# Weight conversion order, zero fillers, 384-token tiles and a new instruction order in a fused attention and two-MoE kernel

## The chip, the cores and the metric

The kernel runs on one core of a Trainium2 chip. The metric is the device time of one execution in microseconds, as the median of several runs. Smaller is better.

## What is computed

Four batches of eight heads of block-causal attention (sequence 576, head size 64, blocks of 64) feed a product chain without a nonlinearity, and that feeds an ELU layer:

```python
scores = where(block_i >= block_j, q @ k.T / 8, -1e9)     # 4 x 8 heads, 576 x 576
x  = softmax(scores) @ v                                  # laid out as 2304 tokens x 512
y  = ((x @ w1) * (x @ w2)) @ w3 @ w_out                   # w1, w2: 512x1024, w3: 1024x1024, w_out: 1024x512
h  = y @ w_in                                             # 512 x 2048
out = where(h > 0, h, exp(min(h, 0)) - 1) @ moe2_w_out    # 2048 x 512
```

Weights arrive as float64 words and are turned into float32 on the core.

## The kernel before, in words

**Numbers.** Most products run in a reduced float32 form on TensorE. Each operand is split into a high part and a rest, and three matmuls (`PASSES`) stand for one product. Two products use whole float32: the transposes of the probabilities, and `w3 @ w_out`.

**Conversion.** `convert` (line 309) turns one unit of 128 x 512 float64 words into float32: a DMA into a raw slot (`cr`, four slots in the first stage), two ScalarE instructions (c0 and c1, lines 354 and 347), three on VectorE (c2, c3, c4, lines 360, 363 and 368), and one on GpSimd (c5, line 377) that writes the finished unit `full`. Units of w1 and w2 get two more instructions that make the two parts. In the first stage there are 8 units of w_out (`wo`), 16 of w3 (`w3T`, two halves for each of 8 row blocks) and 16 of w1 and w2 (`w12`).

**Attention** (line 451). One pair of heads at a time, 16 pairs. A pair loads q, k and v, splits q and k, and has five row groups: scores `s` on TensorE (line 549, the last 64 rows at 611), a maximum on VectorE (570), an exponential on ScalarE (575), transposes `t` on TensorE (585, 645, 654), copies `pt` out of PSUM (439 or 440), and the products with v, `o`, on TensorE (675). The row sums go through a small DRAM buffer `scr` and come back spread over the partitions as `rr` (line 717), by which GpSimd scales the result in `xy` (729, the tile's "n" key).

**The product w3 @ w_out** (`w_product`, line 737). Eight row blocks i of eight terms j each, in PSUM bank 6 or 7. A term is one call of matmul, two matmul records in the trace. Term j of row i waits for both halves of w3's unit i and for both halves of w_out's unit j // 2.

**Block 2** (`block2`, line 776) is the first MoE layer, in 8 tiles of 288 tokens, half a batch each. A tile splits its x into `xs`; for each of 8 m it makes `a` and `b` (line 846, 12 matmuls each, in chunks of 6), multiplies them into `af` (863), and splits that into `g` (769 and 772). After m = 2, 5 and 7 (`PARTS`) the products with the finished w3 @ w_out are added into `xy` (810, copied out at 824 and 830). The first three tiles use one PSUM bank each for a, b and y (5, 6, 7); later tiles use two each, which they share with attention's banks (0, 1 and 3), and so wait until attention is through with these.

**Block 3** (`block3`, line 903) is the ELU layer, in 6 tiles of 384 tokens; `h` at line 918, `o` at 953. Its weights are converted while block 2 runs, once attention's buffers are free (`gate1`, `gate2`).

**The order** is not written by hand. Each instruction group is given to `Plan.add` with an engine, an assumed length and a priority. `Plan.run` walks through time with these lengths: at each step, of the engines' ready groups, it issues the one that can start earliest, with the lowest priority number among equals. The issue order of each engine's queue comes from that, and the chip then runs each queue in order. `TURNS` holds priorities of single groups that replace the usual ones. Usual priorities: the first four pairs -2500, w_out -3000, w3 -1000 + i, w3 @ w_out -2400 + i, w1 and w2 -992, later pairs 10 times their number, block 2 from 10000 on, block 3 from 100000 on; copies out of PSUM near -10000.

**Fillers** (line 1051). Until the first term of w3 @ w_out, `Plan.run` puts matmuls of the mask `mk`, into an unused tile `spare` of bank 6, wherever it sees TensorE idle for longer than 0.3 us: one for each 0.22 us. `mk` is zero but for parts of two rows.

Of the kernel before, what the change touches and what calls it, by code (L numbers as in the profile page):

```python
# [8 lines left out]
F32 = mybir.dt.float32  # L9
# [11 lines left out]
P = 128  # L21
WHOLE = 0
ADDED = 4
HS = 512
T2 = 288
T3 = 384
BIG = 2.0**100
PARTS = ((0, 1, 2), (3, 4, 5), (6, 7))
# [13 lines left out]
COL = 13 / 12 / 2400  # L42
# [166 lines left out]
def attention_moe_moe2(  # L209
# [21 lines left out]
    N2, N3 = B * S // T2, B * S // T3  # L231
# [93 lines left out]
    def convert(src, dst, keys, prio, first):  # L325
# [56 lines left out]
        def c7(eng):  # L382
# [5 lines left out]
            "ACT", 0.68, lambda: c0(nc.scalar), r=[rk], w=[t], prio=prio,  # L388
            ways=[("DVE", 0.42, lambda: c0(nc.vector), True)],
        )  # L390
        add("ACT", 0.68, c1, r=[rk], w=[rk2], prio=prio)
        add(
            "DVE", 0.42, lambda: c2(nc.vector), w=[t], prio=prio, port=True,
        )
        if ps:
            add("DVE", 0.67, c3, r=[t], w=[ps], prio=prio)
            add("DVE", 0.7, c4, r=[rk, ps], w=[t], prio=prio)
        else:
            add("DVE", 0.42, c3, w=[t], prio=prio, port=True)
            add("DVE", 0.7, c4, r=[rk], w=[t], prio=prio, port=True)  # L400
        if len(keys) == 1:
            add("POOL", 1.28, c5, r=[rk2, t], w=keys[0], prio=prio, port=True)
            return
        add("POOL", 1.28, c5, r=[rk2], w=[t], prio=prio, port=True)
        add("ACT", 0.61, lambda: nc.scalar.copy(dst(0), f()), r=[t], w=keys[0], prio=prio)
        add(
            "POOL", 1.28, lambda: c7(nc.gpsimd), r=[t, *keys[0]], w=keys[1], prio=prio, port=True,
# [14 lines left out]
    rr_r = Ring(pool1, "rr", 2, [P, S], F32)  # L422
# [21 lines left out]
    def attention(n, first_op):  # L444
# [42 lines left out]
        else:  # L487
            add("ACT", 0.67, lambda: nc.scalar.copy(qs()[:, 0, :], raw()[:, 0, :]), r=[(raw, 0)], w=[(qs, 0)], prio=pr)
            add(
                "ACT", 0.67,  # L490
# [9 lines left out]
                "DVE", 0.75,  # L500
# [30 lines left out]
        def group(g, seq):  # L531
# [7 lines left out]
            def scores():  # L539
# [20 lines left out]
                "PE", (4 * w / 2390 if whole else 3 * w * COL) + (0.25 if added else 0.12), scores,  # L560
                r=[*q_keys, *k_keys, "mask"], w=[*sb], prio=pg,
            )
            for h in range(2):
# [3 lines left out]
                def top(s=s, c=c):  # L567
# [4 lines left out]
                add("DVE", dve_us(nk) + (0.0 if added else 0.2), top, r=[s], w=[s, (st, "nm", c)], prio=pg)  # L572
                add(
                    "ACT", 0.47 + nk * 0.00083,
# [21 lines left out]
        def last_block(seq):  # L596
# [4 lines left out]
            for g in range(2):  # L601
# [26 lines left out]
                "DVE", 0.16, lambda: nc.vector.tensor_tensor(out=nm(10), in0=nm(8), in1=nm(9), op=ALU.min),  # L628
                r=[(st, "nm", 8), (st, "nm", 9)], w=[(st, "nm", 10)], prio=pg,
            )  # L630
            for g in range(2):
                add(
                    "ACT", 0.47 + kw * 0.00083,
                    lambda g=g: nc.scalar.activation(
                        out=p()[:, g * kw:(g + 1) * kw], in_=sb[g]()[:, 0:kw], func=AF.Exp, bias=nm(10), scale=1.0,
                        accum_out=sm(8 + g),
                    ),
                    r=[sb[g], (st, "nm", 10)], w=[(p, g), (st, "sm", 8 + g)], prio=pg,
                )
# [22 lines left out]
        def pv(c, seq):  # L662
# [20 lines left out]
            add("PE", (0.8, 2.15)[c], product, r=r, w=[o], prio=pg)  # L683
# [21 lines left out]
        add("DVE", 0.75, recip, r=[(st, "rest"), *((st, "sm", c) for c in range(10))], w=[(st, "rs"), rs], prio=pr + 6)  # L705
# [30 lines left out]

    def w_product(i, prio):
        ps = turn("w", (6, 7), "wps")
        for j in range(KF):

            def mm(j=j):
                plan.filler = None
# [13 lines left out]
        add("ACT", 0.58, lambda: nc.scalar.copy(d()[:, 0, :], ps()), r=[ps], w=[k[0]], prio=-9e3)  # L756
        add(
            "DVE", 0.68,
# [16 lines left out]

    def block2(t):
        b, h2 = divmod(t, 2)
        c0 = T2 * h2
# [3 lines left out]
        x = xy[b]  # L782
        for k in range(KD):
            src = lambda k=k: x()[:, k, c0:c0 + T2]
            add(
                "DVE", 0.32, lambda k=k, src=src: nc.vector.tensor_copy(xs()[:, k, 0, :], src()),
                r=[(x, k, "n")], w=[(xs, k, 0)], prio=fast, port=True,
            )
            add(
                "POOL", 0.79,  # L790
                lambda k=k, src=src: nc.gpsimd.tensor_tensor(
                    out=xs()[:, k, 1, :], in0=src(), in1=xs()[:, k, 0, :].bitcast(F32), op=ALU.subtract
                ),
                r=[(x, k, "n"), (xs, k, 0)], w=[(xs, k, 1), (x, k, "s", h2)], prio=fast, port=True,
            )
        gs = []
        few = t < 3
# [3 lines left out]
        def y_part(part):  # L801
            ms = PARTS[part]
            for n in range(KD):
                ps = turn("y" + nm_, ybanks, "y")
                for m in ms:

                    def mm(m=m, n=n, ps=ps):
                        w = wsl(W_S + m // 2).rearrange("p s (j c) -> p s j c", c=DM)[:, :, m % 2, :]
                        for q, (a, c) in enumerate(PASSES):
                            nc.tensor.matmul(  # L810
                                ps()[:, 0:T2], lhsT=w[:, a, n * P:(n + 1) * P], rhs=gs[m]()[:, c, :],
                                start=(m == ms[0] and q == 0), stop=(m == ms[-1] and q == 2),
                            )

                    add(
                        "PE", 3 * T2 * COL + 0.01, mm,
                        r=[(gs[m], 0), (gs[m], 1), *((slab_buf[W_S + m // 2], y, m % 2) for y in range(2))],
                        w=[ps], prio=base + (46, 90, 95)[part] + n, lag=0.5, big=True,
                    )
                d = lambda n=n: x()[:, n, c0:c0 + T2]  # L820
                dk = (x, n, "y", h2)
                if part == 0:
                    add(
                        "ACT", act_us(T2), lambda d=d, ps=ps: nc.scalar.copy(d(), ps()[:, 0:T2]),
                        r=[ps], w=[dk, (x, n, "s", h2)], prio=fast,
                    )
                else:
                    add(
                        "DVE", dve_us(T2),
                        lambda d=d, ps=ps: nc.vector.tensor_tensor(out=d(), in0=ps()[:, 0:T2], in1=d(), op=ALU.add),  # L830
                        r=[ps], w=[dk], prio=fast,
                    )
# [279 lines left out]
```

## Time and profile before

| what | value |
|---|---|
| median of 3 runs | 970.86 us (969.94 to 971.44) |
| profiled execution, own time | 971.84 us |
| its span, first to last instruction | 970.1 us |
| TensorE busy, matmul | 960.6 us (99%) |
| VectorE, ScalarE, GpSimd busy | 511.3, 427.6, 399.2 us |
| mean granted TensorE clock | 0.998 of 2.4 GHz |

Matmuls overlap in their pipeline, so a busy TensorE is not necessarily one that does useful or full-speed work: the mean length of a matmul record holds its latency. How often matmuls start one after the other is read from the start times, or from the length of a long piece of one kind in the chain of waits divided by its count.

### The profile page before, as it was taken

To read this page: it belongs to the slowest core of one execution; us is meant where nothing else is said; L and a number is where in the kernel's file an instruction comes from. 1 tells how busy PE (TensorE), PEld (TensorE's weight loads), DVE (VectorE), ACT (ScalarE), POOL (GpSimd) and SP (SyncE) were. 2 spreads that over 40 slices of the span, in tenths; PEclk is the share of its full clock that TensorE was granted. 3 is DMA by queue.
4 is the path that set the end of the run, shared out by engine and by line. 5 is a ranking of instruction groups with operands and counts; after the bars stand their busy time and mean duration, and the time that the engine had idled before them with its cause. 6 is when DMAs were issued, how large, how long until landed. Compare 5 with 4: busy or idle time off the path is not lost.

```text
span 970.1 us, 15899 instructions
## 1 busy us (share of the span) xinstructions
PE 960.6 (99%) x5910; PEld 821.4 (85%) x5910; DVE 511.3 (53%) x1087; ACT 427.6 (44%) x1008; POOL 399.2 (41%) x419
## 2 busy tenths in 40 slices
PE   9999999999999999999999999999999999999998
PEld 4555478788888889999999999998999889888997
DVE  7888988766565556676766342322322322322322
ACT  5867577556656654464454422222222222222222
POOL 6354758323232226666656542332322422422222
PEclk9999999999999999999999999999999999999999
DMA  8554433131122003245465950000000000000000
GB/s 290 195 184 161 160 128 96 54 96 50 50 78 71 27 16 112 95 154 183 171 210 202 391 233 1 1 32 1 23 12 1 25 10 1 33 1 1 33 1 33
DMA packets 41789, 87.61 MB, mean 90 GB/s; under 512 B 6000, under 2 KB 15472, under 8 KB 40176
## 3 DMA queue, kind: packets, MB, share of 16 engines
q1 hardware_dynamic: 41712, 86.60, 25.8%
q8 instruction: 46, 0.75, 0.3%
q14 instruction: 31, 0.25, 0.1%
HBM read 69.21 MB, written 17.38 MB: 89 GB/s over the span
## 4 chain that ended last, share of the span: by engine, by line
PE 93%; DVE 4%; DMA 1%; issue 1%; SPq 1%; POOL 0%; ACT 0%; POOLq 0%; DVEq 0%; ACTq 0%
PE h L918 21%; PE o L953 21%; PE b L846 10%; PE a L846 10%; PE y L810 10%; PE o L675 5%; PE s L549 4%; PE t L585 4%; PE wps L745 4%; PE spare L1054 3%; PE s L611 1%; DVE ct L368 1%; DVE ct L360 1%; PE t L645 1%; DMA scr<-rs 0%
## 5 line engine op out<-in xcount | busy, mean ns | idle before, releaser
L772 POOL TENSOR_TENSOR g<-e,g 128x384 fp32r<-128x384 f32 x96 | 97.4, 1016 | 276.6 <-ACT g L769 262.8
L930 DVE TENSOR_SCALAR e<-h 128x384 f32<-128x384 f32 x96 | 53.4, 557 | 221.6 <-PE h L918 210.1
L953 PE MATMUL o<-slab_lo,g 128*128 128x512 f32 x648 | 162.9, 396 | 0.0
L934 ACT ACTIVATE e<-e 128x384 f32<-128x384 f32 x96 | 50.4, 525 | 232.2 <-DVE e L930 232.2
L953 PEld LDWEIGHTS o<-slab_lo,g 128*128 128x128 f32 x648 | 121.1, 188 | 23.5
L810 PE MATMUL y<-g,slab_lo 128*128 128x288 f32 x768 | 118.9, 300 | 0.5 <-DVE xy L830 0.3
L846 PE MATMUL a<-xs,slab_lo 128*128 128x288 f32 x768 | 117.9, 298 | 0.0
L846 PE MATMUL b<-xs,slab_lo 128*128 128x288 f32 x768 | 117.1, 297 | 0.4 <-DVE af L863 0.4
L810 PEld LDWEIGHTS y<-g,slab_lo 128*128 128x128 f32 x768 | 106.5, 188 | 2.7 <-issue 1.0
L846 PEld LDWEIGHTS b<-xs,slab_lo 128*128 128x128 f32 x768 | 106.7, 188 | 1.4 <-DVE af L863 0.6
L846 PEld LDWEIGHTS a<-xs,slab_lo 128*128 128x128 f32 x768 | 106.9, 188 | 1.0 <-issue 0.3
L772 POOL TENSOR_TENSOR g<-af,g 128x288 fp32r<-128x288 f32 x64 | 56.0, 875 | 80.0 <-ACT g L769 78.4
L918 PE MATMUL h<-xb,slab_lo 128*128 128x384 f32 x432 | 82.1, 339 | 0.0
L918 PE MATMUL h<-xa,slab_lo 128*128 128x384 f32 x432 | 81.5, 336 | 0.0
L939 DVE SCALAR_TENSOR_TENSOR e<-e,h 128x384 f32<-128x384 f32 x96 | 53.1, 554 | 51.2 <-ACT e L934 50.9
L918 PEld LDWEIGHTS h<-xb,slab_lo 128*128 128x128 f32 x432 | 77.1, 188 | 3.0
L918 PEld LDWEIGHTS h<-xa,slab_lo 128*128 128x128 f32 x432 | 76.3, 188 | 3.2 <-DVE e L939 0.2
L769 ACT CAST g<-e 128x384 fp32r<-128x384 f32 x96 | 49.0, 513 | 66.2 <-DVE e L939 58.2
L374 POOL TENSOR_TENSOR ct<-ct,cr 128x512 int32<-128x512 int32 x48 | 65.2, 1362 | 30.3 <-DVE ct L368 11.5
L575 ACT ACTIVATE p<-s,st 128x128 f32<-128x128 f32 (+3 forms) x128 | 67.2, 528 | 16.1 <-DVE st L570 11.4
L570 DVE TENSOR_REDUCE st<-s 128x1 f32<-128x128 f32 (+3 forms) x128 | 61.4, 489 | 5.5 <-PE s L555 2.1
L439 ACT COPY pt<-t 128x512 f32<-128x512 f32 (+4 forms) x91 | 36.8, 409 | 55.9 <-PE t L585 49.1
(89 smaller groups left out, 1455.7 us busy)
## 6 DMA issues: line engine op xcount, KB each, us to landing
cr<-w SPq DMA_DIRECT2D x48, 512.0 KB
wsc<-stage SPq DMA_DIRECT2D x24, 512.0 KB
slab_lo<-wsc SPq DMA_DIRECT2D x12, 1024.0 KB
cr<-w3T SPq DMA_DIRECT2D x16, 512.0 KB
raw<-qT SPq DMA_DIRECT2D x16, 288.0 KB
raw<-kT SPq DMA_DIRECT2D x16, 288.0 KB
out<-ob SPq DMA_DIRECT2D x17, 256.0 KB
cr<-wo SPq DMA_DIRECT2D x8, 512.0 KB
```

The costliest lines, as they stand in the source:

```text
L374: nc.gpsimd.tensor_tensor(out=t(), in0=t(), in1=words()[0], op=ALU.add)
L570: nc.vector.tensor_reduce(out=nm(c), in_=s()[:, 0:nk], axis=AX.X, op=ALU.max, negate=True)
L575: lambda s=s, c=c, p=p: nc.scalar.activation(out=p()[:, 0:nk], in_=s()[:, 0:nk], func=AF.Exp, bias=nm(c), scale=1.0, accum_out=sm(c)),
L769: add("ACT", act_us(n, True), lambda: nc.scalar.copy(g()[:, 0, :], src()), r=[key], w=[(g, 0)], prio=prio)
L772: lambda: nc.gpsimd.tensor_tensor(out=g()[:, 1, :], in0=src(), in1=g()[:, 0, :].bitcast(F32), op=ALU.subtract),
L810: nc.tensor.matmul(ps()[:, 0:T2], lhsT=w[:, a, n * P:(n + 1) * P], rhs=gs[m]()[:, c, :], start=(m == ms[0] and q == 0), stop=(m == ms[-1] ...
L846: nc.tensor.matmul(ps()[:, 0:T2], lhsT=w[:, a, u, k, :], rhs=xs()[:, k, c, :], start=(k == 0 and q == 0), stop=(k == KD - 1 and q == 2),)
L918: nc.tensor.matmul(ph()[:, 0:T3], lhsT=w[:, a, k, :], rhs=xs()[:, k, c, :], start=(k == 0 and q == 0), stop=(k == KD - 1 and q == 2),)
L930: "DVE", dve_us(T3), lambda e=e, ph=ph: nc.vector.tensor_scalar_min(e(), ph()[:, 0:T3], 0.0),
L934: "ACT", act_us(T3, True), lambda e=e: nc.scalar.activation(out=e(), in_=e(), func=AF.Exp),
L939: lambda e=e, ph=ph: nc.vector.scalar_tensor_tensor(out=e(), in0=e(), scalar=-1.0, in1=ph()[:, 0:T3], op0=ALU.add, op1=ALU.max),
L953: nc.tensor.matmul(acc(), lhsT=g()[:, a, s * P:(s + 1) * P], rhs=w[:, c, :], start=(m == 0 and q == 0), stop=(m == KG - 1 and q == 2),)
```

## The change

Of w_out and w3, units are converted in another order: the two halves of w_out's unit 0, the first half of w3's rows 0 and 1, w_out's unit 1, the second half of w3's rows 0 and 1, w_out's units 2 and 3, and then the rest of w3 row by row. A term of w3 @ w_out waits only for that half of w3 that it reads. The four w3 units of rows 0 and 1 get the priority of w_out.

Fillers multiply a tile of zeros and write to the bank of the first row of w3 @ w_out; between its terms they add zeros to the sum. They end with that row's last term instead of with its first.

Block 2 has 6 tiles of 384 tokens, cut as block 3's. Tiles 1 and 4 so lie across two batches, in two pieces of 192. `PARTS` becomes four pairs; `g` has 4 buffers where it had 6, and `af` one for two; two tiles, not three, keep to one bank each. `rr` has one buffer for two. The assumed lengths of `Plan` are changed throughout, and `TURNS` is another table.

```diff
-T2 = 288
-T3 = 384
-PARTS = ((0, 1, 2), (3, 4, 5), (6, 7))
+TT = 384
+FEW = 2
+PARTS = ((0, 1), (2, 3), (4, 5), (6, 7))
+YPRIO = (36, 56, 90, 95)
-COL = 13 / 12 / 2400
+COL = 1.0945 / 2400
 TURNS = {
...
-    LAT = {"GATE": 0.0, "PE": 0.25, "DVE": 0.12, "ACT": 0.12, "POOL": 0.12, "SP": 0.0}
+    LAT = {"GATE": 0.0, "PE": 0.25, "DVE": 0.155, "ACT": 0.175, "POOL": 0.12, "SP": 0.0}
...
-    rr_r = Ring(pool1, "rr", 2, [P, S], F32)
+    rr_r = Ring(pool1, "rr", 1, [P, S], F32)
+    zero = p1.tile([P, P], BF16, name="zero")
     def act_us(n, sbuf=False):
-        return (0.19 if sbuf else 0.16) + n * 0.00083
+        return (0.11 if sbuf else 0.08) + n * 0.00083
     def dve_us(n):
-        return 0.145 + n * 0.00105
+        return 0.085 + n * 0.00105
...
+    first_w = []
     def w_product(i, prio):
         ps = turn("w", (6, 7), "wps")
+        if i == 0:
+            first_w[:] = [ps, False]
             def mm(j=j):
-                plan.filler = None
+                if i == 0:
+                    first_w[1] = True if j < KF - 1 else None
-                r=[*full_keys(W3_S, i % RW), *full_keys(WO_S, j // 2)], w=[ps], prio=prio, big=True,
+                r=[full_keys(W3_S, i % RW)[j // 4], *full_keys(WO_S, j // 2)], w=[ps], prio=prio, big=True,
-    xs2_r = Ring(pool2, "xs", 1, [P, KD, 2, T2], F32R)
-    g2_r = Ring(pool2, "g", 6, [P, 2, T2], F32R)
-    a2_r = Ring(pool2, "af", 2, [P, T2], F32)
+    xs2_r = Ring(pool2, "xs", 1, [P, KD, 2, TT], F32R)
+    g2_r = Ring(pool2, "g", 4, [P, 2, TT], F32R)
+    a2_r = Ring(pool2, "af", 1, [P, TT], F32)
...
-        few = t < 3
+        few = t < FEW
...
+    for s in range(4):
+        for h in range(2):
+            wo_unit(s, h)
+        if s < 2:
+            for i in range(2):
+                w3_unit(i, s, -3000.0)
...
+        nc.gpsimd.memset(zero, 0.0)
     def filler(n):
+        ps, begun = first_w
+        if begun is None:
+            return
         for _ in range(n):
             nc.tensor.matmul(
-                spare[0], lhsT=mk, rhs=mk.rearrange("p (a c) -> p a c", a=1).to_broadcast([P, 4, P]), start=True, stop=True
+                ps(), lhsT=zero, rhs=zero.rearrange("p (a c) -> p a c", a=1).to_broadcast([P, 4, P]),
+                start=not begun, stop=not begun,
             )
```

## Rows read from the trace of the kernel before

**Rows 1.** Page, first part: busy us, share of the span, instructions.
```profile
PE 960.6 (99%) x5910; PEld 821.4 (85%) x5910; DVE 511.3 (53%) x1087; ACT 427.6 (44%) x1008; POOL 399.2 (41%) x419
```
**Rows 2.** Page, chain that ended last: share of the span by engine.
```profile
PE 93%; DVE 4%; DMA 1%; issue 1%; SPq 1%; POOL 0%; ACT 0%; POOLq 0%; DVEq 0%; ACTq 0%
```
**Rows 3.** TensorE's waits up to 130 us: us in total, times, longest.
```profile
PE t L585 <- ACT p L575: 1.8, 1, 1.8
```
**Rows 4.** Busy time by stage: window, length, engines' busy us (instructions), clock, DMA.
```profile
0.00:128.00 128.00, 124.22 (x601) 64.23 (x601) 106.17 (x202) 87.05 (x201) 72.05 (x82) 0.99 0.60 199
128.00:361.40 233.40, 232.25 (x1805) 193.34 (x1803) 156.37 (x435) 142.98 (x414) 86.23 (x102) 1.00 0.20 62
361.40:563.70 202.30, 201.82 (x1508) 201.29 (x1505) 128.01 (x225) 93.20 (x192) 122.22 (x112) 1.00 0.54 195
```
**Rows 5.** TensorE's groups up to 32.6 us: count, busy us, mean ns, idle before.
```profile
L1054 PE MATMUL spare<-mk 128*128 128x512 bf16 x102 | 25.3, 410 | 2.0 <-POOL mk L982 2.0
```
**Rows 6.** Timeline of the start: start us, length, engine, line, operation.
```profile
10.68 1.36 POOL L377 TENSOR_TENSOR full<-ct,cr 128x512 int32<-128x512 int32 x1 [0.42 <-ACT q L488]
...
14.58 1.39 POOL L377 TENSOR_TENSOR full<-ct,cr 128x512 int32<-128x512 int32 x1
...
18.19 1.35 POOL L377 TENSOR_TENSOR full<-ct,cr 128x512 int32<-128x512 int32 x1 [0.43 <-ACT ct L354]
...
31.26 1.29 POOL L377 TENSOR_TENSOR full<-ct,cr 128x512 int32<-128x512 int32 x1 [0.43 <-ACT cr L347]
...
32.73 1.88 PE L745 MATMUL wps<-full,full 128*128 128x512 f32 x4
```
**Rows 7.** Chain in order of time: start us, length us, piece.
```profile
108.42 19.08 PE wps L745 x44
157.19 2.42 PE o L675 x20
...
359.07 2.42 PE o L675 x20
...
476.39 5.60 PE y L810 x42
...
598.45 2.10 PE h L918 x12
...
632.04 2.12 PE h L918 x12
```
**Rows 8.** TensorE's groups up to 361.42 us, block 2's three.
```profile
L846 PE MATMUL b<-xs,slab_lo 128*128 128x288 f32 x288 | 46.1, 300 | 0.4 <-DVE af L863 0.4
L846 PE MATMUL a<-xs,slab_lo 128*128 128x288 f32 x288 | 45.6, 301 | 0.0
L810 PE MATMUL y<-g,slab_lo 128*128 128x288 f32 x237 | 41.0, 309 | 0.0
```
**Rows 9.** Waits of all engines up to 380 us: GpSimd's scaling step.
```profile
POOL xy L729 <- DMA rr<-scr: 57.9, 14, 9.9
```
**Rows 10.** Groups of the whole span by shape, TensorE's y and steps behind it.
```profile
L810 PE MATMUL y<-g,slab_lo 128*128 128x288 f32 x768 | 118.9, 300 | 0.5 <-DVE xy L830 0.3
...
L772 POOL TENSOR_TENSOR g<-e,g 128x384 fp32r<-128x384 f32 x96 | 97.4, 1016 | 276.6 <-ACT g L769 262.8 <-issue 13.8
...
L939 DVE SCALAR_TENSOR_TENSOR e<-e,h 128x384 f32<-128x384 f32 x96 | 53.1, 554 | 51.2 <-ACT e L934 50.9
...
L769 ACT CAST g<-e 128x384 fp32r<-128x384 f32 x96 | 49.0, 513 | 66.2 <-DVE e L939 58.2 <-PE o L953 8.0
...
L830 DVE TENSOR_TENSOR xy<-y,xy 128x288 f32<-128x288 f32 x64 | 28.7, 453 | 19.7 <-PE y L810 19.4
```
**Rows 11.** Busy time in 4 us windows around TensorE's one long wait.
```profile
70.00:74.00 4.00, 2.21 (x6) 0.66 (x5) 2.88 (x5) 1.28 (x4) 3.56 (x4) 1.00 0.74 252
74.00:78.00 4.00, 3.99 (x21) 2.49 (x23) 3.69 (x7) 3.43 (x8) 2.62 (x2) 0.68 0.66 227
78.00:82.00 4.00, 4.00 (x19) 2.00 (x16) 2.59 (x6) 2.28 (x6) 1.08 (x1) 0.89 0.44 159
```

More of the change, by code (lines that the diff above doesn't have):

```diff
@@ L704, in attention @@
         add("POOL", 0.15, lambda: nc.gpsimd.memset(st()[:, 41:64], 0.0), w=[(st, "rest")], prio=pr)
-        add("DVE", 0.75, recip, r=[(st, "rest"), *((st, "sm", c) for c in range(10))], w=[(st, "rs"), rs], prio=pr + 6)
+        add("DVE", 0.72, recip, r=[(st, "rest"), *((st, "sm", c) for c in range(10))], w=[(st, "rs"), rs], prio=pr + 6)
         def keep_sums(b):
@@ L774, in split_g, with pieces, split_x, xs_keys @@
         )
+    def pieces(t):
+        a0, out_ = t * TT, []
+        while a0 < (t + 1) * TT:
+            b, o = divmod(a0, S)
+            n = min(S - o, (t + 1) * TT - a0)
+            out_.append((b, o, n, a0 - t * TT))
+            a0 += n
+        return out_
+    def split_x(t, xs, kind, done, fast):
+        for k in range(KD):
+            for b, o, n, d0 in pieces(t):
+                key = (xy[b], k, "n") if kind == "n" else (xy[b], k, "y", t)
+                src = lambda b=b, o=o, n=n, k=k: xy[b]()[:, k, o:o + n]
+                add(
+                    "DVE", 0.09 + n * 0.00052,
+                    lambda k=k, d0=d0, n=n, src=src: nc.vector.tensor_copy(xs()[:, k, 0, d0:d0 + n], src()),
+                    r=[key], w=[(xs, k, 0, d0)], prio=fast, port=True,
+                )
+                add(
+                    "POOL", 0.17 + n * 0.00215,
+                    lambda k=k, d0=d0, n=n, src=src: nc.gpsimd.tensor_tensor(
+                        out=xs()[:, k, 1, d0:d0 + n], in0=src(), in1=xs()[:, k, 0, d0:d0 + n].bitcast(F32), op=ALU.subtract
+                    ),
+                    r=[key, (xs, k, 0, d0)], w=[(xs, k, 1, d0), *([(xy[b], k, "s", t)] if done else [])], prio=fast,
+                    port=True,
+                )
+    def xs_keys(t, xs, k0):
+        return [(xs, k, c, p[3]) for k in (k0, k0 + 1) for c in range(2) for p in pieces(t)]
     def block2(t):
-        b, h2 = divmod(t, 2)
-        c0 = T2 * h2
         xs = xs2_r.next()
@@ L781, in block2 @@
         fast = -1e4 + t
[L782 to L795, printed above, removed]
+        split_x(t, xs, "n", True, fast)
         gs = []
-        few = t < 3
+        few = t < FEW
         abanks, bbanks, ybanks = ((5,), (6,), (7,)) if few else ((5, 0), (6, 1), (7, 3))
@@ L815, in y_part @@
                     add(
-                        "PE", 3 * T2 * COL + 0.01, mm,
+                        "PE", 3 * TT * COL + 0.01, mm,
                         r=[(gs[m], 0), (gs[m], 1), *((slab_buf[W_S + m // 2], y, m % 2) for y in range(2))],
-                        w=[ps], prio=base + (46, 90, 95)[part] + n, lag=0.5, big=True,
+                        w=[ps], prio=base + YPRIO[part] + n, lag=0.5, big=True,
                     )
[L820 to L832, printed above, removed]
+                for b, o, nt, d0 in pieces(t):
+                    d = lambda b=b, o=o, nt=nt, n=n: xy[b]()[:, n, o:o + nt]
+                    dk, src = (xy[b], n, "y", t), lambda d0=d0, nt=nt, ps=ps: ps()[:, d0:d0 + nt]
+                    if part == 0:
+                        add(
+                            "ACT", act_us(nt), lambda d=d, src=src: nc.scalar.copy(d(), src()),
+                            r=[ps], w=[dk, (xy[b], n, "s", t)], prio=fast,
+                        )
+                    else:
+                        add(
+                            "DVE", dve_us(nt),
+                            lambda d=d, src=src: nc.vector.tensor_tensor(out=d(), in0=src(), in1=d(), op=ALU.add),
+                            r=[ps], w=[dk], prio=fast,
+                        )
         for m in range(KF):
@@ L923, in block3 @@
                 add(
-                    "PE", 6 * T3 * COL, mm,
-                    r=[*wk, *((xs, k, c, p[3]) for k in (k0, k0 + 1) for c in range(2) for p in pieces)],
+                    "PE", 6 * TT * COL, mm,
+                    r=[*wk, *xs_keys(t, xs, k0)],
                     w=[ph], prio=base + 10 * m, lag=0.3, big=True,
@@ L960, in block3 @@
             ob = late["ob"].next()
-            r0 = t * T3 + s * P
-            end = t == N3 - 1 and s == T3 // P - 1
+            r0 = t * TT + s * P
+            end = t == NT - 1 and s == TT // P - 1
             for h in range(2 if end else 1):
@@ L1009, in attention_moe_moe2 @@
     for i in range(KF):
-        for h in range(2):
-            c = slice(h * HS, (h + 1) * HS)
-            convert(
-                w3T[i][:, c], lambda x, i=i, c=c: full(W3_S, i % RW)[:, c], [[full_keys(W3_S, i % RW)[h]]], cp + i, True
-            )
+        if i > 1:
+            for h in range(2):
+                w3_unit(i, h, cp + i)
         w_product(i, -2400.0 + i)
@@ L1020, in attention_moe_moe2 @@
     n1 = len(plan.ops)
-    for t in range(N2):
+    for t in range(NT):
         block2(t)
@@ L1042, in attention_moe_moe2 @@
             )
-    late["e"] = t2_ring.share("e", [P, T3], F32)
+    late["e"] = t2_ring.share("e", [P, TT], F32)
     late["ob"] = cr2_ring.share("ob", [P, DM], F32)
-    for t in range(N3):
-        block3(t, *(first3[t] if t < 2 else block3_in(t)))
-    spare = []
+    for t in range(NT):
+        block3(t, first3[t] if t < 2 else block3_in(t))
     def filler(n):
-        if not spare:
-            spare.append(psum.tile([P, 512], F32, name="spare", tag="bank6"))
+        ps, begun = first_w
+        if begun is None:
+            return
         for _ in range(n):
             nc.tensor.matmul(
-                spare[0], lhsT=mk, rhs=mk.rearrange("p (a c) -> p a c", a=1).to_broadcast([P, 4, P]), start=True, stop=True
+                ps(), lhsT=zero, rhs=zero.rearrange("p (a c) -> p a c", a=1).to_broadcast([P, 4, P]),
+                start=not begun, stop=not begun,
             )
```

123 lines of the change are left out of this document (51 added, 72 removed), and 36 rows, old and new, of the table TURNS.

## The prediction

> **What bounds the kernel now.** I read the page's busy shares first: TensorE has a matmul under way in 960.6 of 970.1 us, and no other engine is above 53% [rows 1]. The chain of waits says the same: 93% of it lies on TensorE [rows 2]. A busy record does not prove useful work, so the next view is TensorE's waits. Up to 130 us two matter: 2.0 us at the very start [rows 5] and one of 1.8 us [rows 3]. Then the stages: until 128 us VectorE is busy for 106 us of 128 and ScalarE for 87; until attention's end at 361.4 us VectorE for 156 of 233 and ScalarE for 143; in the stage behind it both are below two thirds [rows 4]. So the length is TensorE's own work, plus what fills it without use. The unneeded part is named by the groups of the start: 102 filler matmuls, 25.3 us, all before the first term of w3 @ w_out at 32.7 us [rows 5, 6]. The kernel gets shorter by what takes the fillers' place, by what makes the matmuls themselves shorter, and longer by each new moment in which TensorE has nothing to do.
>
> **The start: order of conversion, half dependencies.** A finished unit is the end of GpSimd's instruction at line 377. Units 3, 4, 6 and 10 end at 12.0, 16.0, 19.5 and 32.6 us [rows 6] (the others lie between, one in some 1.8 us where nothing comes between them). Before, a term needs w_out's two halves and both halves of w3, and the order gives all eight w_out units first, so the first term stands behind unit 10. In the new order, at the same pace:
> - unit 3 (w3 row 0, first half) frees two terms of row 0 at 12.0 us, unit 4 two of row 1 at 16.0
> - unit 6 frees the two next terms of both rows at 19.5 us: four
> - unit 8 frees none; unit 10 frees four at 32.6 us, unit 12 the last four.
>
> So eight terms run before 32.6 us where none did, in place of fillers. A term is two records; 44 in one piece take 19.08 us [rows 7], 0.867 us a term. 8 x 0.867 = 6.9 us. The bounds: nothing, if the units come later than before; 16 terms, 13.9 us, if the twelve units now ahead in priority come faster at the cost of attention's first pairs. I take 6.9, since the old pace already holds attention's share. Work that leaves the start is not there later: the last 22 terms now run in one piece of 19.1 us at 108.4 us [rows 7], and behind them block 2 must come in earlier. GpSimd's extra memset for the zeros is at the start, with the others, under the first DMA; I count nothing.
>
> **The fillers.** They write zeros in place of a mask that is nearly all zero itself, and run in gaps of `Plan`'s own time line, some of them now between terms. They cost when the chip's gap is shorter than planned: at 0.22 us each, a handful, 1 us. They save when a gap would have cost clock. I take nothing.
>
> **384-token tiles.** Before: 42 matmuls of 288 columns in 5.60 us, 133.3 ns each; 12 of 384 columns in 2.10 us early and 2.12 us late in block 3 [rows 7], 175.0 to 176.7 ns. Block 2 has 8 x 288 = 2304 of the former, 307.2 us, and will have 6 x 288 = 1728 of the latter: 302.4 to 305.3 us. It saves 1.9 to 4.8 us; I take the middle, 3.4, because block 2's place is next to the early part. A rule speaks for less. The Trainium skill, "TensorE: Matmul & The Clock Gate", section "Wait — 56ns, not 53.3ns?", gives each matmul a fixed 2.5 ns beside its columns; an estimate from that page is 576 matmuls fewer x 2.5 ns = 1.4 us, which would make the sum 2.0 us smaller. The trace differs: 288 columns at 2.4 GHz are 120 ns and take 133.3.
>
> **Smaller rings.** With one `af`, ScalarE's copy of the next a waits for GpSimd's last use. Behind b come a multiplication, a cast and a subtraction: for 384 columns 0.554 + 0.513 + 1.016 = 2.08 us [rows 10] and hand-offs, while the next a takes 12 x 0.176 = 2.11 us. The copy is late by the hand-offs, but its bank is wanted only after the next b, another 2.11 us on: nothing, and if GpSimd is a whole scaling step late that cover is just used up. With four `g`, the fifth waits for the first y part, which precedes it on TensorE by priority: nothing. The copies out of PSUM rise from 96 to 128 (four parts, two tiles in two pieces); 32 x 0.453 us [rows 10] is 14.5 us of VectorE, which is idle for 74 of the 202 us behind attention [rows 4]: nothing there. One `rr`: a pair's fetch waits for the scaling before it, in SP's queue, with later loads behind it. GpSimd now waits 57.9 us for fetches [rows 9], at worst 9.9 us, against 18.4 us between two pairs ((359.07 - 157.19) / 11 [rows 7]): nothing.
>
> **The reserve.** The largest unknown. Until attention ends, TensorE's gaps are filled by those tiles that keep to banks 5 to 7. Before, that was three of 288, 864 matmuls, and 813 had run by 361.4 us [rows 8]: 108.4 us, nearly all. Now it is two of 384, 576 x 0.1758 = 101.3 us. The rest of the program behind attention's end is 970.1 - 361.4 = 608.7 us; without its 1491 old matmuls (198.8 us) 409.9, with 1152 new ones (202.5 us) 612.4. So the span is attention's end + 612.4 us: no gain if it ends at 357.7, and 959.8 if TensorE stays full, which means an end at 361.4 - 6.9 - (108.4 - 101.3) = 347.4 us, 14 us sooner. From 128 us on, 12 pairs leave VectorE idle for 77 us and ScalarE for 90 [rows 4], so there is room. I take TensorE as full, as it is in the stage of before, and count the shortfall at nothing; its other end is 14 us.
>
> **The sum.** 970.1 - 6.9 - 3.4 = 959.8 us of span. The profiled execution took 971.84 us, 1.74 over its span, so 961.5 like it; the median of the runs is 0.98 below the profiled one: 970.86 - 10.3 = **960.6 us**.
>
> **Rivals.**
>
> First: the start does not do what it says. Twelve units are ahead of attention, the raw slots are four, and SP issues in order; if w3's first units come after 25 us, the eight terms do not run early. For: unit 4 came 3.9 us behind unit 3 [rows 6]. Against: the place in the order is what decides. Only the tiles remain: 970.86 - 3.4 = 967.5 us.
>
> Second, the other side: attention does not end sooner. Its groups precede block 2 by priority already, so 18.4 us a pair may be the pace of its chain through three engines, not TensorE's. A chunk of six matmuls now holds TensorE for 1.05 us where it was 0.80, and a ready attention group waits for half of that, 0.13 us more, at some 17 groups a pair, and 12 pairs: up to 26 us, against the 14 to be gained. Then the two tiles run out, and TensorE stands still. With attention's end where it is, 361.4 + 612.4 = 973.8 us, 974.6 as a median. It decides from an end later than 357.7 us. Against: without chunks in the way the pairs run faster, which gives part of it back.
>
> Third: single banks for y. A tile has 16 y groups of 1.05 us for 12 of 1.2 (tiles of 288 before), and in two tiles all go through bank 7, so each waits for the copy before it unless attention fills in. Before, TensorE waits for such a copy for 0.3 us in all [rows 10]. Uncovered, eight groups at a tile's end cost some 0.55 us of copy [rows 10] and a hand-off each, 6 us, and the clock: behind the 1.8 us wait of before the granted clock was 0.68 for 4 us and 0.89 for 4 more [rows 11], 1.7 us lost. One tile's end: 960.6 + 8 = 969 us; both, 977. The Trainium skill, "TensorE: Matmul & The Clock Gate", section "A second HAM failure mode: psum-queue depth-cycling", tells of such short idles between groups; by that rule, which the trace bears out with these two windows, a loss of clock comes on top of the idle time.
>
> **How the numbers follow.** The forecast has 0.50, with 949 (13.9 at the start, 4.8 by the tiles, the old wait and its clock, 3.5, gone) to 966 (part of the reserve missing); the first rival 0.13; the second 0.24, 971 to 978; the third 0.13, 967 to 977. About 0.2%, 1.9 us, can be told from no change: 968.9 and 972.8 are the bounds. Faster: 0.50 + 0.12 of the first + 0.05 of the third = 0.67. The same: 0.01 of the first, 0.05 of the second, 0.04 of the third, 0.10. Slower: 0.19 of the second and 0.04 of the third, 0.23. The range is 949 to 976 us.
>
> **What would show it.** Right: first term near 12 us and eight before the pace of 32 us; fewer than some 75 fillers (a term takes the place of four); block 2 near 176 ns a matmul, 304 us in all; attention's last o near 347 us, and behind it some 612 us. The first rival shows as a first term after 25 us, the second as waits of TensorE on attention's tiles before its end, with the end behind 357 us, the third as waits of y on VectorE's copies and granted clock under 1 at the same place. A new wait behind attention, or block 3 at another length than before, would make the sum wrong in a place that I do not count.

## The result and the profile after

The changed kernel takes **981.9 us** (median of 4 runs, 981.31 to 982.81); before took 970.4 us (969.92 to 971.44) on the same chip. The ratio is 1.0118, 95% interval 1.0100 to 1.0135: slower by 11.5 us, where I forecast 960.6 us and a range up to 976.

The page's first part and its chain by engine, of the changed kernel, answer to [rows 1, 2].

```profile
PE 956.5 (98%) x5294; PEld 812.3 (83%) x5294; DVE 532.1 (54%) x1106; ACT 426.2 (44%) x982; POOL 384.2 (39%) x395
...
PE 77%; DVE 12%; DMA 5%; ACT 2%; issue 2%; POOL 2%; SPq 0%; POOLq 0%; ACTq 0%; DVEq 0%
```

TensorE has less to do, 956.5 against 960.6 us, in a span that grew from 970.1 to 979.5 us. So it stands more, and the chain names for whom: VectorE's share rose from 4% to 12%, that of transfers from 1% to 5%. An average says no more than that; the stages say where. The same three windows as [rows 4], the bounds moved to the changed kernel's attention end (362.4) and block 3 (573.5):

```profile
0.00:128.00 128.00, 119.30 (x565) 61.37 (x566) 111.89 (x209) 89.58 (x204) 69.52 (x80) 0.99 0.60 199
128.00:362.40 234.40, 227.53 (x1564) 183.36 (x1562) 158.28 (x436) 138.74 (x398) 76.14 (x89) 0.99 0.20 62
362.40:573.50 211.10, 207.67 (x1165) 205.23 (x1166) 140.40 (x236) 93.23 (x178) 121.10 (x103) 1.00 0.55 196
```

Attention ends at 362.4 us, not at 347.4 as forecast and not much later than the 361.4 of before. Until there TensorE stands 15.6 us of 362.4 (362.4 - 119.3 - 227.5), against 4.9 of 361.4 before. Behind it the program needs 979.5 - 362.4 = 617.1 us where 612.4 were forecast. These are the two misses: 15.0 + 4.7 = 19.7 us of span.

Next, what TensorE waits for. First up to attention's end, then in the stage behind it (us in total, times, longest):

```profile
PE t L585 <- ACT p L575: 9.4, 8, 2.3
PE s L549 <- ACT p L575: 2.1, 2, 1.3
...
PE t L585 <- DVE pt L440: 1.6, 1, 1.6
...
PE y L832 <- DVE xy L853: 3.3, 5, 1.0
```

The row of [rows 3], one wait of 1.8 us, has become eight with 9.4 us together: a transposition wants p, the exponentials that ScalarE writes. Behind attention y waits for VectorE's additions, 3.3 us, where 0.3 us stood before [rows 10].

The start does what the change says. TensorE's groups up to 32.6 us, and the timeline of the first terms, against [rows 5, 6]:

```profile
L1063 PE MATMUL wps<-zero 128*128 128x512 bf16 x62 | 16.6, 431 | 1.7 <-POOL zero L981 1.7
L750 PE MATMUL wps<-full,full 128*128 128x512 f32 x17 | 8.3, 605 | 0.0
```
```profile
12.40 1.68 POOL L376 TENSOR_TENSOR full<-ct,cr 128x512 int32<-128x512 int32 x1 [0.44 <-issue]
...
14.78 3.60 PE L750 MATMUL wps<-full,full 128*128 128x512 f32 x8
...
108.26 18.29 PE L750 MATMUL wps<-full,full 128*128 128x512 f32 x42
```

62 fillers for 102, and 16 records (eight terms) before 32.6 us where none ran; the seventeenth starts the next terms at 32.43 us. But the last term ends at 108.26 + 18.29 = 126.6 us; before it ended at 108.42 + 19.08 = 127.5 [rows 7]. Of 6.9 us won at the start 0.9 are left 95 us later.

Where they went shows in the chain of waits of the first 175 us. In before a third of that chain is w3 @ w_out's terms and fillers (20.3% and 14.2%). In the changed kernel it runs, for its first 45 us, almost without TensorE (start us, length us, piece):

```profile
14.11 4.25 DMA cr<-w3T
18.44 0.69 ACT cr L346
19.13 1.28 POOL full L376
20.42 5.14 DMA cr<-wo
26.83 0.66 PE s L549 x4
27.67 1.01 DVE st L570 x2
28.68 0.61 DVE ct L359
29.32 0.70 DVE cp L362
30.05 0.69 DVE ct L367
...
43.59 3.59 DMA cr<-w3T
```

It is the loop of the conversions: a load into one of four raw slots, ScalarE, VectorE's three steps, GpSimd's addition, and only then the slot's next load. Attention's small steps hang in the same VectorE queue. One place in full, VectorE, then ScalarE and TensorE:

```profile
127.78 0.69 DVE L367 SCALAR_TENSOR_TENSOR ct<-cr,ct 128x512 int32<-128x512 int32 x1
128.38 0.42 DVE L359 TENSOR_SCALAR ct<-ct 128x512 f32<-128x512 f32 x1
128.84 0.43 DVE L362 TENSOR_SCALAR ct<-ct 128x512 int32<-128x512 int32 x1
129.30 0.69 DVE L367 SCALAR_TENSOR_TENSOR ct<-cr,ct 128x512 int32<-128x512 int32 x1
129.99 0.11 DVE L569 MEMSET s<- 64x64 f32 x1
130.14 0.29 DVE L570 TENSOR_REDUCE st<-s 128x1 f32<-128x128 f32 x1
```
```profile
130.53 0.37 ACT L575 ACTIVATE p<-s,st 128x128 f32<-128x128 f32 x1 [2.96 <-DVE st L570]
```
```profile
128.73 0.69 PE L869 MATMUL a<-xs,slab_lo 128*128 128x384 f32 x3
131.04 0.33 PE L585 MATMUL t<-ident,p 128*128 128x128 f32 x1 [1.62 <-ACT p L575]
132.01 0.33 PE L585 MATMUL t<-ident,p 128*128 128x128 f32 x1 [0.65 <-ACT p L575]
...
132.83 0.44 PE L869 MATMUL a<-xs,slab_lo 128*128 128x384 f32 x1
```

VectorE works through four conversion steps before the maximum that p needs; ScalarE stands 2.96 us for it, and TensorE 1.62 us and 0.65 us for p, although the rest of the a group (the last row) has its inputs (the last piece of `xs` was written at 118.7 us): it stands behind the transposition in TensorE's queue, whose order was fixed when the program was written. Such a wait costs clock too:

```profile
133.00:137.00 4.00, 4.00 (x16) 3.86 (x16) 3.22 (x10) 3.28 (x8) 1.49 (x1) 0.57 0.88 280
```

The four microseconds from 133 us on, behind these waits of 1.62 and 0.65 us, have a granted clock of 0.57 of 2.4 GHz, close to the lower of the two levels (1.2 GHz), 1.72 us lost. [rows 11] showed the same of before. The Trainium skill's "TensorE: Matmul & The Clock Gate", section "A second HAM failure mode: psum-queue depth-cycling", tells of clock lost to short idles between groups of matmuls, there while PSUM banks are cycled. The trace agrees as to the loss; the idle here is a wait for p.

### The profile page after: what moved, and what is told of

Its sections match the earlier page's. It is cut to its first block, busy times and chain, and to the rows that moved or that the text cites. A ratio compares the mean times of both kernels' runs of the same rounds, so it can differ in the third digit from the quotient of the medians.

```text
span 979.5 us, 14676 instructions
## 1 busy us (share of the span) xinstructions
PE 956.5 (98%) x5294; PEld 812.3 (83%) x5294; DVE 532.1 (54%) x1106; ACT 426.2 (44%) x982; POOL 384.2 (39%) x395
## 4 chain that ended last, share of the span: by engine, by line
PE 77%; DVE 12%; DMA 5%; ACT 2%; issue 2%; POOL 2%; SPq 0%; POOLq 0%; ACTq 0%; DVEq 0%
PE h L918 21%; PE o L953 21%; PE y L832 8%; PE a L869 8%; PE b L869 8%; PE o L675 4%; PE s L549 3%; PE t L585 3%; DVE ct L367 2%; DMA cr<-w3T 2%; DVE ct L359 2%; DMA cr<-w 2%; DVE xs L798 1%; DVE ct L362 1%; PE s L611 1%
## 5 line engine op out<-in xcount | busy, mean ns | idle before, releaser
L832 PE MATMUL y<-g,slab_lo 128*128 128x384 f32 x576 | 118.3, 344 | 3.4 <-DVE xy L853 3.3
L869 PE MATMUL a<-xs,slab_lo 128*128 128x384 f32 x576 | 115.5, 342 | 0.0
L869 PE MATMUL b<-xs,slab_lo 128*128 128x384 f32 x576 | 114.4, 343 | 0.0
L832 PEld LDWEIGHTS y<-g,slab_lo 128*128 128x128 f32 x576 | 99.9, 188 | 7.6 <-DVE xy L853 4.3
L869 PEld LDWEIGHTS b<-xs,slab_lo 128*128 128x128 f32 x576 | 102.2, 189 | 1.8 <-issue 0.7
L869 PEld LDWEIGHTS a<-xs,slab_lo 128*128 128x128 f32 x576 | 101.5, 188 | 1.2 <-issue 0.2
L777 POOL TENSOR_TENSOR g<-af,g 128x384 fp32r<-128x384 f32 x48 | 53.8, 1121 | 56.1 <-ACT g L774 49.5
L585 PE MATMUL t<-ident,p 128*128 128x128 f32 x320 | 55.4, 283 | 11.1 <-ACT p L575 9.4
```

The source lines that it names most:

```text
L585: nc.tensor.transpose(d[:, j, :], p()[:, j * P:(j + 1) * P], ident)
L777: lambda: nc.gpsimd.tensor_tensor(out=g()[:, 1, :], in0=src(), in1=g()[:, 0, :].bitcast(F32), op=ALU.subtract),
L832: nc.tensor.matmul(ps()[:, 0:TT], lhsT=w[:, a, n * P:(n + 1) * P], rhs=gs[m]()[:, c, :], start=(m == ms[0] and q == 0), stop=(m == ms[-1] ...
L869: nc.tensor.matmul(ps()[:, 0:TT], lhsT=w[:, a, u, k, :], rhs=xs()[:, k, c, :], start=(k == 0 and q == 0), stop=(k == KD - 1 and q == 2),)
```

## The experiments

Theories: **V**, the pace of the first 175 us is that of VectorE and of the loads before it, and a TensorE queue of fixed order passes each lateness on; **T**, TensorE is full there, as the prediction had it, and the change lost elsewhere; **O**, the parts are sound, and it is the written order (lengths, landing times, table of turns) that doesn't fit the chip. All times are medians; before, measured again beside each group of runs, took 971.1, 970.8, 971.8 and 971.5 us. The changed kernel's 981.9 us stands beside 970.4, so a difference from it is good to about 1 us.

**Less work on VectorE.** The clamp, one of VectorE's steps per unit, is left out of the 40 conversions of the first stage; order and all else stay.

```diff
         def c2(eng):
+            if first:
+                return
             a = t().bitcast(F32)
```

> The kernel after with the instruction order of every engine as it is, but the clamp (third step) of the 40 units of w_out, w3, w1 and w2 left out on VectorE; the weights lie inside the clamp's bounds. VectorE theory (until about 175 us attention and the conversions are paced by VectorE, and TensorE stands behind attention's tiles in its fixed order): VectorE loses some 40 x 0.6 us, attention's end moves from 362 us to 350 or 355 us, the time from 981.9 to 968 to 976 us. TensorE theory (the loss is in TensorE's own work: less of block 2 ahead of attention's end, y copies): within 2 us of 981.9.

> The kernel before with the same 40 clamps left out, order kept. VectorE theory: its order is less crowded there (83% busy up to 128 us), so the gain is smaller than in the kernel after: 2 to 5 us, 965 to 968 us. TensorE theory: 970.4, as TensorE has no waits to lose but one of 1.8 us.

Measured: 969.15 us (968.22 to 972.51) in the changed kernel, 12.8 less than with the steps; 967.74 us (966.47 to 968.42) in before, 3.4 less. The steps are the same 40 x 0.42 = 16.8 us of VectorE in both (0.6 each was expected). The changed kernel gets three quarters of them back, with attention's last o at 351.0 us: in the order as it is written most of the pace hangs on VectorE, which is V. Before gets a fifth, and had little more to gain: its TensorE stood 4.7 us up to 175 us, 2.0 of them at the very start, and a granted clock of 0.98 from 32.6 to 128 us cost 1.9. In the changed kernel TensorE's waits for p up to 362 us fell from 9.4 to 7.1 us, and those of s and for pt are all but gone:

```profile
PE t L587 <- ACT p L577: 7.1, 6, 2.7
...
PE s L551 <- ACT p L577: 0.6, 2, 0.3
```

The waits are not all of it. The granted clock rose with them, from 0.98 to 1.00 between 32.6 and 128 us and from 0.96 to 1.00 between 128 and 175 us: 1.9 us each.

**Less work on TensorE.** Seven of eight terms of one row of w3 @ w_out are left out, the conversions stay.

```diff
-                nc.tensor.matmul(ps(), lhsT=a[:, j, :], rhs=bb, start=(j == 0), stop=(j == KF - 1))
+                if i != 1 or not j:
+                    nc.tensor.matmul(ps(), lhsT=a[:, j, :], rhs=bb, start=(j == 0), stop=(i == 1 or j == KF - 1))
```

> The changed kernel, its order and table as they are, with seven of the eight terms of row 1 of the product w3 w_out left out on TensorE (14 matmuls of 128x512, some 0.44 us each, 6.2 us in the first 60 us); their conversions stay. Theory (VectorE, the loads and the fixed order set the pace of the first 175 us, TensorE waits there anyway): within 1.5 us of the changed kernel, 980.4 to 983.4. Rival (TensorE is full, the step the prediction took): 6 us less, 975 to 977.

> The same seven terms left out of the kernel before. Theory (as above, with some slack left: TensorE waited 1.8 us at the longest group there): 0 to 3 us less, 968 to 971. Rival (TensorE is full there): 6 us less, 964 to 965.

Measured: 980.63 us (978.89 to 983.74) for 981.9, and 969.94 us (969.05 to 972.45) for 971.8. Of 6.2 us taken from TensorE 1.3 us came back in the changed kernel (2.6 when each time is held against before beside it) and 1.8 in before. T is out, and with it the step "I take TensorE as full, as it is in the stage of before". The clean case is before: its TensorE idles 8.9 us up to attention's end instead of 4.9, at the same granted clock, and its waits of t for p, 1.8 us with the terms, are now

```profile
PE t L585 <- ACT p L575: 4.1, 4, 1.9
```

A share of 97% [rows 4] did not show that matmuls lay where TensorE would otherwise have waited. In the changed kernel idle time up to 362.4 us grows by only 1.4 us. More went into the clock: s waits once for 2.6 us near 25 us, and the four microseconds from 28 us on, at 1.00 in the changed kernel, have 0.58:

```profile
PE s L549 <- ACT p L575: 3.3, 2, 2.6
```
```profile
28.00:32.00 4.00, 4.00 (x19) 2.20 (x17) 3.86 (x8) 3.05 (x9) 1.43 (x1) 0.58 0.65 224
```

With 0.91 from 40 to 60 us, also 1.00 in the changed kernel, that is 3.5 us of lost clock in the profiled execution. So a_drop alone would be weak evidence against T; b_drop is the better one.

**The table of turns.** Both kernels with an empty table: the order then comes from priorities and lengths alone.

```diff
-TURNS = {
...
-}
+TURNS = {}
```

> The kernel after with an empty table of replaced priorities; lengths, tiles and conversion order as they are. Theory that the structure is sound and the order is to blame: without a table on either side the kernel after is the faster one, by 3 us or more. Theory that the structure costs (reserve, y copies): it is slower than the kernel before without its table, by some 10 us, as with the tables. Both expect 985 to 1005 us here.

> The kernel before with an empty table of replaced priorities. Both theories: slower than with the table, 980 to 1005 us; what counts is how it stands to the kernel after without its table.

Measured: 985.74 us (984.47 to 988.69) and 1005.81 us (1003.94 to 1007.52). Without tables the changed kernel is 20 us faster than before. The table is worth 35 us in before and 4 us in the changed kernel. That points to O: old parts in an order that fits the chip well, new parts in one that does not. It does not show it, since the two also plan with different lengths and an order without a table is one of many; the new tables below decide.

**The lengths, without a table.** The change shortened the planned lengths to those of back-to-back neighbours. But c3 reads what c2 wrote, c4 what c3 wrote, on the same engine. VectorE in the changed kernel, one unit:

```profile
6.83 0.42 DVE L359 TENSOR_SCALAR ct<-ct 128x512 f32<-128x512 f32 x1
7.28 0.69 DVE L362 TENSOR_SCALAR cp<-ct 128x512 int32<-128x512 int32 x1
8.01 0.69 DVE L367 SCALAR_TENSOR_TENSOR ct<-cr,cp 128x512 int32<-128x512 int32 x1
8.62 0.42 DVE L359 TENSOR_SCALAR ct<-ct 128x512 f32<-128x512 f32 x1
```

A step that needs the one before starts 0.03 to 0.04 us after its end (6.83 + 0.42, then 7.28), one that doesn't 0.08 us before it (8.01 + 0.69, then 8.62). The three take 1.79 us; the old lengths say 0.42 + 0.67 + 0.70 = 1.79, the new ones 0.37 + 0.62 + 0.62 = 1.61. First the plan got 0.11 us more for such pairs, then all the old lengths came back, both with an empty table.

```diff
-u.ready = max(u.ready, o.end + (0.0 if [*u.ways] == [e] != ["SP"] else self.LAT[e] + u.lag))
+u.ready = max(u.ready, o.end + ((0.0 if e == "PE" else 0.11) if [*u.ways] == [e] != ["SP"] else self.LAT[e] + u.lag))
```

> The changed kernel with an empty table, its plan told that a step on VectorE, ScalarE or GpSimd which reads its own engine's last result starts 0.11 us later. To be held against the changed kernel with an empty table, 985.74 (984.47 to 988.69), where the plan has 0 there. Theory (the lengths are right for neighbours and wrong for chains, and the order made from them is what makes TensorE wait): 975 to 982. Rival (the lengths don't matter, without a table the order is poor anyway): 984 to 988.

> The changed kernel with an empty table and every length of before put back (three VectorE steps of a unit 0.42, 0.67 and 0.70 = 1.79 us, which is also what the trace shows for the chain). Theory of the lengths: the old ones leave the slack that the chains need, so 975 to 983 against 985.74 with the new ones. Rival: no difference, 984 to 988. If it is slower than 988 the back-to-back lengths were the better ones and the loss is the table's alone.

Measured: 989.2 us (988.86 to 993.98) and 984.34 us (983.44 to 989.22), against 985.74. My theory of the lengths fails here: the more faithful plan gave the slower order, and the old lengths change nothing that counts (held against before without its table, 1005.81 us, the changed parts are 21 us ahead at equal lengths). An order made without a table moves by some microseconds whichever number is touched, so this pair can't weigh the lengths.

**A table that fits.** The 0.12 us above stays in, and TURNS is replaced by a table found by many trials of changed turns on the plan's own time line, each also with lengths and landings some per cent off, so that no turn is right by a hair only. The kernel before got the new lengths, the same correction and a table in the same way.

```diff
 TURNS = {
-    14: -2528.99, 30: -2548.11, 48: -2482.05, 54: -3229.71, 65: -2493.16, 66: -2502.23, 68: -2501.39, 74: -3235.7,
+    3: -99931.4713, 4: -99515.8136, 15: -2419.1506, 17: -3006.0017, 24: -106784.8336, 37: -6868.8706, 39: -1138.8531, 42: -2584.4547,
...
 }
```

(448 entries in a_tab, 446 in b_tab, where the changed kernel has 117 and before 131.)

> The changed kernel's parts, with two things replaced: its plan adds 0.12 us where a step on VectorE, ScalarE or GpSimd reads what its own engine has just written (the trace after has c2 to c3 to c4 start 0.46, 0.73 and 0.60 us apart where the lengths of the change assume 1.61 us for the three), and a table of turns found against those lengths. Theory (what was lost is order: VectorE has no slack in the plan, and TensorE stands in its fixed queue behind steps that come late): of the 18.1 us that TensorE waits for other engines in the trace after (9.4 and 1.6 for p and pt, 3.3 for y's copies, 2.1 and 1.7) at least two thirds go, so 981.9 - 12 to 16 = 966 to 970, below the kernel before, attention's last o before 352. Rival (the changed kernel has too much work on VectorE in the first 175 us for any order; 12.8 us came only when 40 of its steps were left out): no order helps, 978 to 984, attention's last o still at about 360.

> The kernel before with the changed kernel's lengths, the same 0.12 us, and a table found in the same way: its start, its 288-token tiles and its single xy's are as they were. Theory (the parts of the change are worth what their rows said, about 3.4 us of cadence and 7 us of start, once the order fits): 8 to 10 us above the run a_tab, so 974 to 980 if that is 966 to 970. Rival (the parts are worth nothing and a better table would have helped either kernel): within 3 us of a_tab.

Measured: 971.4 us (969.4 to 973.38) and 976.0 us (974.12 to 977.38). The changed kernel won 10.5 us, less than the 12 to 16 expected, and the parts of the change are 4.6 us ahead, between the 3 and the 8 to 10 of the two theories. Before did not gain from its new table: 976.0 us is above its own 970.8. What may still be missing shows in ScalarE's waits for transfers, first 175 us of a_tab:

```profile
ACT cr L385 <- DMA cr<-w: 8.6, 9, 3.9
ACT cr L385 <- DMA cr<-w3T: 7.3, 6, 2.5
```

and in one load, SP's queue and its reader:

```profile
63.71 0.58 SPq L424 DMA_DIRECT2D cr<-w3T  x1
...
69.41 0.66 ACT L385 ACTIVATE cr<-cr 128x512 int32<-128x512 uint32 x1 [2.46 <-DMA cr<-w3T]
```

Issued at 63.71, used at 69.41, with ScalarE idle for it: 5.7 us, where the plan has 3.54.

**Loads that land later in the plan.** Two tables, a_tab3 and a_tab4, were made anew with this.

```diff
-                pipe = max(pipe, t + 1.9) + o.nbytes / 390e3
-                o.end, free[e] = pipe + 0.3, t + 0.45
+                pipe = max(pipe, t + 2.2) + o.nbytes / 330e3
+                o.end, free[e] = pipe + 0.4, t + 0.45
```

> As the run a_tab (the changed kernel's parts, another table, 0.12 us for a step that reads its own engine's last result), with one thing more in the plan: transfers land later. In a_tab ScalarE alone stood 25 us for the 512 KB loads of the conversions in the first 175 us (8.6, 7.3, 4.1, 3.7 and 1.3 us), because a load that the plan expects after 3.54 us was used 4 to 6 us after its issue; now 2.2 us to the first byte, 330 instead of 390 KB per us, 0.4 instead of 0.3 us at the end, and a table found against that. Theory (late loads are what the plan of a_tab left out): the table keeps most of what its plan promises, 958 to 966. Rival (no order helps, the first 175 us are full of work on VectorE): 969 to 974 as a_tab.

> A second table found in the same way as that of a_tab3, all else the same: it shows how much of a time is the one table's chance. Theory: within 4 us of a_tab3, 958 to 966. Rival: 969 to 974.

Measured: **964.8 us** (963.16 to 967.82), ratio to before 0.9937, interval 0.9914 to 0.9959, and 966.61 us (965.08 to 970.49), 0.9952, 0.9939 to 0.9965. Both beat both kernels; a_tab3 is the version to keep. Its chain, three stages (attention ends at 352.7, block 3 begins at 555.9) and TensorE's longest wait up to attention's end and the one behind it:

```profile
PE 84%; DVE 7%; DMA 4%; ACT 1%; issue 1%; POOL 1%; SPq 1%; POOLq 0%; ACTq 0%; DVEq 0%
```
```profile
0.00:128.00 128.00, 121.51 (x620) 65.90 (x621) 113.24 (x236) 94.66 (x229) 77.85 (x88) 1.00 0.64 204
128.00:352.70 224.70, 222.56 (x1523) 180.40 (x1521) 147.18 (x410) 126.96 (x368) 75.68 (x86) 0.99 0.20 62
352.70:555.90 203.20, 201.99 (x1144) 201.04 (x1143) 127.89 (x240) 90.50 (x173) 121.23 (x103) 1.00 0.56 200
```
```profile
PE t L683 <- ACT p L672: 1.9, 2, 1.7
...
PE y L870 <- DVE xy L891: 1.2, 2, 0.8
```

TensorE stands 352.7 - 121.5 - 222.6 = 8.6 us up to attention's end instead of 15.6, attention ends 9.7 us sooner, and y waits 1.2 us instead of 3.3. Some 23 more matmuls of block 2 (600 for 577, 4 us) have run by then, and the stage behind is 7.9 us shorter. VectorE does as much in the first 128 us as in the changed kernel (113.2 against 111.9 us), and the parts are the same: the gain is one of order, which is O. Order here is more than sequence: `Plan.run` also chooses the engine of those steps that may run on two (`ways`), and over the whole span VectorE has 510.2 us of work for 532.1. That it does the urgent things first I infer; no run separates that from the choice of engine. ScalarE's waits for the loads of w and w3T, the two rows above, fell to 4.1 and 2.1 us.

**Which correction, and what the parts are worth.** a_tab5 has the later loads without the 0.12 us; b_tab3 and b_tab4 are the old parts with both corrections and a table each.

> The changed kernel's parts with the later landing of loads in the plan and a table found against it, but without the 0.12 us for a step that reads its own engine's last result. Theory L (the late loads are the missing cost): 963 to 968, as a_tab3 and a_tab4. Theory V (both are needed, VectorE's chains are 0.18 us a unit longer than the plan's lengths): 969 to 975. If a_tab's 971.4 came from a poor table alone, this one tells nothing of L.

> The kernel before, its start, 288-token tiles and single xy's as they were, with the changed kernel's lengths, both corrections and a table found in the same way as that of a_tab3. Theory (the change's parts are worth some 5 to 8 us when the order is made with equal care, as a_tab against b_tab, 971.4 to 976.0): 970 to 974. Rival (a better order helps before as much, the parts are worth nothing): 963 to 967.

> A second table for the kernel of b_tab3, for the one table's chance. Theory: 970 to 974. Rival: 963 to 967.

Measured: 968.99 us (966.85 to 970.54); 973.49 us (971.47 to 976.62) and 969.27 us (968.19 to 970.56), the last in neither range. a_tab5 lies between steps alone (971.4) and both (964.8, 966.6), on the border of its two theories, and two tables of one kind differ by 1.8 and 4.2 us: each correction seems to help, how much each stays open. Nor was a table of some 440 entries made against the change's own lengths, so how much of the gain is the larger table alone stays open too; in before the larger table with the first correction lost 5 us. The old parts reach 971.4 us in the mean of two tables, the new ones 965.7: the parts of the change are worth some 6 us with tables made in the same way (2.7 to 8.7 by single pairs), about half of the 10.3 forecast.

## Why the prediction was wrong, step by step

- **The start** (-6.9): right in what it does. First terms at 14.78 us, not 12, since unit 3 ended at 14.1; eight terms early; 62 fillers, under the 75 named. So the first rival, a first term after 25 us, did not come. The gain was given back before 127 us. That the work "is not there later" holds only if TensorE is what the later stage waits for.
- **384-token tiles** (-3.4): right. Behind attention's end groups of twelve come 2.12 us apart, 176.7 ns a matmul, which is the edge of the range with the smaller gain, 1.9 us.
```profile
375.15 2.28 PE L869 MATMUL a<-xs,slab_lo 128*128 128x384 f32 x12
377.27 2.28 PE L869 MATMUL b<-xs,slab_lo 128*128 128x384 f32 x12
```
- **Fillers, memset, small rings, one `rr`** (nothing): no row of TensorE's waits contradicts that, but for the copies out of PSUM counted under the rings. y waits for them 3.3 us behind attention, where 0.3 us stood, although VectorE is idle for a third of that stage.
- **The reserve, the step that failed.** "I take TensorE as full, as it is in the stage of before, and count the shortfall at nothing; its other end is 14 us." Attention's end missed by 15.0 us, all of that other end. TensorE's idle time grew by 15.6 - 4.9 = 10.7 us. The granted clock from 128 to 175 us, 0.96 in place of 1.00, is another 1.9; the remaining 2.4 us I can't place. That stretch in the changed kernel, then in before:
```profile
128.00:175.00 47.00, 41.63 (x266) 34.77 (x265) 40.26 (x91) 31.69 (x84) 23.30 (x24) 0.96 0.27 85
128.00:175.00 47.00, 46.13 (x350) 40.36 (x349) 41.02 (x98) 34.38 (x95) 31.11 (x31) 1.00 0.29 96
```
I read VectorE's room as a mean from 128 us on; the waits lie mainly between 30 and 175 us (7.7, 1.3 and 1.6 us of the three rows shown first above), where VectorE has conversions and attention in one queue. Its amount of work is not what differs (40.3 against 41.0 us in these lines; a_tab3 has more in the first 128 us and waits less), the order is. b_drop shows the step false by itself.
- **The second rival** was right in half. Attention does not end sooner, 362.4 for 361.4 us, and TensorE waits on attention's tiles before that, as its sign said; "the pace of its chain through three engines" fits the late p. Its price does not: 974.6 us, measured 981.9. It had attention groups held up behind longer chunks; in the place shown a chunk stands behind an attention group. And it had two tiles run out; by 362.4 us 210 matmuls of a and 198 of b had run, and two tiles have 192 of each, so the third had begun, and from 175 us on TensorE stood only 1.5 us.
- **The third rival** did not come where it was priced, in the two tiles whose y has one bank. Their y did not wait up to attention's end (the last figure is idle time before it), nor in their last groups up to 373 us:
```profile
L832 PE MATMUL y<-g,slab_lo 128*128 128x384 f32 x169 | 38.3, 353 | 0.0
```
The five waits of y, 3.3 us, come from 405 us on, in tiles that have two banks. a_tab3 has 1.2 us with the same banks, so the order sets them. Of the 4.7 us lost behind attention they are 3.0 more than before; 1.0 is cadence (1152 x 0.9 ns), 0.7 is open.
- **What I did not price** was the table. I treated the order of some 3,700 steps as given and reckoned with work; the empty tables show 35 us of before's time hanging on it, and new ones took 10 to 17 us off the changed kernel's.

## What to carry over

A stage in which one engine is 97% busy need not be bound by it, if another engine's queue decides when its next input comes: take a few microseconds of its work away, see what comes back, and read the granted clock beside it. When a program's order is written from a plan, a change of parts is also a change of how well that order fits; price the order before crediting the parts, by emptying its table in both kernels (good to some microseconds) and by making it anew in both. And put into such a plan what the trace shows at the places where engines wait: the time from a load's issue to its use, and the step that reads its own engine's last result. Here that and the larger tables together were worth 15 to 17 us.

## What the hardware showed that I had not expected

- A 512 KB load held the chain of the changed kernel for 3.6 to 5.9 us from its issue (3.59, 4.25 and 5.14 us above, 5.85 from 70.32 us on); the plan of both kernels has 3.54 us for one alone. What made some longer no run isolates.
- On VectorE a step that reads its predecessor's result starts 0.03 to 0.04 us after that one's end, an independent one mostly 0.08 or 0.09 us before it, in the first 130 us of the changed kernel: 0.11 to 0.13 us a pair, on steps of 0.42 to 0.69 us.
- 16.8 us of VectorE work taken out were worth 12.8 us in the changed kernel and 3.4 us in before, a granted clock that rose by 0.02 to 0.04 included.
- Work taken out of TensorE can cost it clock: in a_drop 3.5 of 6.2 us went that way.
